# The low half of the split weights: a negated copy on ScalarE and an accumulating DMA in place of VectorE's subtraction

## The chip, the core and the metric

The kernel runs on one core of one Trainium2 chip. The metric is the time of one execution on the device, in microseconds (us); lower is better. One execution was recorded by the hardware profiler, and its times of single instructions are used here. Instruction times, windows and starts are counted from the first instruction of that execution.

The engines go by the names of the profile: PE is TensorE (PEld its weight loads), DVE is VectorE, ACT is ScalarE, POOL is GpSimd, SP is SyncE, which here only issues DMAs.

## The reference

A linear recurrence over 768 steps of time for 4 batches and 8 heads of 48 channels, and a dense layer with GELU behind it:

```python
for t in range(S):
    kt, vt, rt = (k[:, :, t], v[:, :, t], r[:, :, t])
    cur = np.einsum('bhd,bhe->bhde', u[None] * kt, vt)
    y[:, :, t] = np.einsum('bhd,bhde->bhe', rt, state + cur)
    state = w[None, :, :, None] * state + np.einsum('bhd,bhe->bhde', kt, vt)
x = y.transpose(0, 2, 1, 3).reshape(B * S, H * D)      # 3072 x 384
h = x @ w_in                                           # 384 x 2048, float64
g = 0.5 * h * (1.0 + erf(h * inv_sqrt2))
out = (g @ w_out).astype(np.float32)                   # 2048 x 384, float64
```

The two weight matrices come as 64-bit floats. The kernel turns them into 32-bit floats on the chip, and splits each into a high half that TensorE's fp32r format holds and a low half that is the rest.

## The kernel before

**Tiling.** Time is cut into 6 tiles of 128 steps; a tile holds 4 batches x 128 steps = 512 tokens (`TOK`). The hidden dimension of the dense layer is cut into 16 blocks of 128 (`NJ`). So the dense layer has 6 x 16 = 96 steps `m`, of which the first 16 (tile 0) run while the weights are still being prepared. The recurrence is done in 24 groups, 6 tiles x 4 pairs of heads; groups 0 to 3 come first, the others are spread over the steps, one group to four steps.

**One step of the dense layer** (`moe1` and `moe2`, the matmuls in lines 602 and 642). `product1` makes `Hp` = w_in block times x in nine matmuls of 128 x 512: three with the high weights `wh` and the high half of x, three with the low weights `wl`, three with `wh` and the low half of x. ScalarE reads `Hp` twice, L630 writes `gh` (GELU, rounded to fp32r) and L631 writes `gf` (GELU in 32 bits); VectorE makes `gl = gf - gh` in L632. `product2` adds nine more matmuls into the banks `O0` to `O2`: `wh` with `gh`, `wl` with `gh`, `wh` with `gl`.

**The weights** (`w_load` and `w_split`), once for each of the 16 blocks, in tile 0 alone; the results stay in SBUF for all tiles. SP loads block `j` into `raw` (three buffers, 128 x 768 values of 64 bits, L317). ScalarE makes the magnitude from the high word (L330, into `wa`, three buffers) and converts the low word (L332, into `wb`, two buffers). VectorE shifts (L334), sets the sign (L336) and adds the low bits (L338); then `wa` holds the 32-bit weights. ScalarE copies them into `wh` (L340, the write rounds to fp32r), and VectorE subtracts: `wl = wa - wh` (L342). The next user of the same `wa` buffer is L330 of block `j + 3`.

**A group of the recurrence** (`prepare`, `products`, `state`, `past_scores`, `finish`): SP loads `Tb` (L208) and `Nb` (L212); VectorE scales `Tb` (L479) and sums (L491); POOL multiplies `Nb` three times (L482, L485, L488); TensorE runs L519, L527, L536 and L546; ScalarE writes `Am` in eight pieces of 128 x 64 (L351) and the high half of x (L367); VectorE updates the states (L569), selects (L576) and writes the low half of x (L368). `Nb` has two buffers; the load of one waits for the matmuls of L546 of the group that used it, two groups before.

**What sets the order.** The class `Plan` takes every operation with an engine, a cost in nanoseconds and a due time, plays them through once at build time, and writes each engine's queue in the order in which its model starts them: the ready operation that is due first. Each queue then runs in that fixed order on the chip; an instruction whose input is late holds up all that stand behind it on its engine. An operation whose due time is `LATER` inherits it from those that need it. So a change of one operation's engine or cost reorders the queues of all engines.

Of the kernel before, what the change touches and what calls it, by code (L numbers as in the profile page):

```python
# [9 lines left out]
F32 = mybir.dt.float32  # L10
# [3 lines left out]
AF = mybir.ActivationFunctionType  # L14
ALU = mybir.AluOpType
# [20 lines left out]
LATER = 10 ** 7  # L36
# [10 lines left out]
class Plan:  # L47
# [9 lines left out]
    def add(self, eng, ns, at, fn, r=(), w=()):  # L57
        n = len(self.ops)
        deps = set()
        for x in r:  # L60
            deps.add(self.writer.get(x))
            self.readers.setdefault(x, []).append(n)
        for x in w:
            deps.add(self.writer.get(x))
            deps.update(self.readers.pop(x, ()))
            self.writer[x] = n
        deps -= {None, n}
        self.ops.append((eng, ns, at, fn, deps))
        self.reads.append(set(r))
# [65 lines left out]
def rwkv_gelu_mlp(tc, rkT, rkv, wuT, uN, wmlp, r, k, vT, w, u, out):  # L135
    nc = tc.nc
    with ExitStack() as ctx:
# [7 lines left out]
        def sb(shape, dt, name, pool=None):  # L145
            return (pool or wk).tile(shape, dt, name=name)
# [11 lines left out]
        wh = [sb([128, 2, DM], F32R, f"wh{j}", cst) for j in range(NEAR)]  # L158
        wl = [sb([128, 2, DM], F32R, f"wl{j}", cst) for j in range(NEAR)]
# [33 lines left out]
        add, dma = plan.add, plan.dma  # L193
        dve = lambda n: 65 + n / 0.96
        dve2 = lambda n: 65 + n / 1.92
        act = lambda n: 95 + n / 1.2
        sdve = lambda n: 145 + n / 0.96
        sdve2 = lambda n: 145 + n / 1.92
        sact = lambda n: 225 + n / 1.2
        pool = lambda n: 110 + n * 2.15  # L200
# [28 lines left out]
        for dst, src, x in ((diag2, diag, "diag"), (past2, past, "past")):  # L229
            for h in range(2):  # L230
                add("act", 280, LATER, lambda dst=dst, src=src, h=h: nc.scalar.copy(
                    out=dst[64 * h:64 * h + 64], in_=src[64 * h:64 * h + 64, 64 - 64 * h:128 - 64 * h]),
                    r=[x], w=[f"{x}2{h}"])
# [86 lines left out]
        def w_split(j):  # L320

            a, b = wa[j % 3], wb[j % 2]
            A_, B_, R_ = f"wa{j % 3}", f"wb{j % 2}", f"raw{j % 3}"
            bits = raw[j % 3].rearrange("p h n t -> p (h n) t")
            lo, hi = bits[:, :, 0], bits[:, :, 1]
            af = a.bitcast(F32)
            gate = ["late"] if j >= NEAR else []
            n = 2 * DM
            both = lambda w: w[j].rearrange("p h n -> p (h n)")
            add("act", sact(n), LATER, lambda: nc.scalar.activation(out=af, in_=hi.bitcast(F32), func=AF.Abs,  # L330
                                                                scale=2.0 ** -112), r=[R_], w=[A_])
            add("act", sact(n), LATER, lambda: nc.scalar.activation(out=b, in_=lo.bitcast(U32), func=AF.Copy,  # L332
                                                                scale=2.0 ** -29), r=[R_], w=[B_])
            add("dve", sdve2(n), LATER, lambda: nc.vector.tensor_scalar(  # L334
                out=a, in0=a, scalar1=3, scalar2=None, op0=ALU.logical_shift_left), w=[A_])
            add("dve", sdve(n), LATER, lambda: nc.vector.scalar_tensor_tensor(  # L336
                out=a, in0=hi, scalar=-2 ** 31, in1=a, op0=ALU.bitwise_and, op1=ALU.bitwise_or), r=[R_], w=[A_])
            add("dve", sdve(n), LATER, lambda: nc.vector.tensor_tensor(out=a, in0=a, in1=b, op=ALU.add),  # L338
                r=[B_], w=[A_])
            add("act", sact(n), LATER, lambda: nc.scalar.copy(out=both(wh), in_=af), r=[A_] + gate,  # L340
                w=[f"wh{2 * j}", f"wh{2 * j + 1}"])
            add("dve", sdve(n), LATER, lambda: nc.vector.tensor_tensor(  # L342
                out=both(wl), in0=af, in1=both(wh).bitcast(F32), op=ALU.subtract),
                r=[A_, f"wh{2 * j}", f"wh{2 * j + 1}"] + gate, w=[f"wl{2 * j}", f"wl{2 * j + 1}"])


        def bonus(am, AM, diag, DIAG, n, sums, CS, j, e):
# [432 lines left out]
        for G in range(NSTEP + 1):  # L780
            if 0 <= G < NJ:
                if G >= 3:
                    w_load(G, step_at(G) - WEIGHT_AHEAD)
                w_split(G)
            if G < NSTEP:
                moe1(G, step_at(G))
            if G == 0:
                group(NP, LATER)
            if G % 4 == 0 and G // 4 + NP < NG:
                gi = G // 4 + NP + 1  # L790
                at = step_at(4 * (gi - 1 - NP)) + GROUP_DUE
                if 5 < gi < NG:
                    load_group(gi, at - GROUP_AHEAD)
                group(gi, at)
            if G >= 1:
                moe2(G - 1, step_at(G) + 2000, out[(G - 1) // NJ])
            if G == 2 * NJ:
                count_plain(step_at(G))
# [96 lines left out]
```

## Time and profile before

| | |
|---|---|
| median of 3 runs | 512.32 us (511.55 to 515.15) |
| the profiled execution | 512.43 us, of which 510.7 us is the span from the first to the last instruction |
| PE busy | 488.2 us, 96% of the span |
| PEld busy | 387.8 us, 76% |
| DVE busy | 248.8 us, 49% |
| ACT busy | 213.6 us, 42% |
| POOL busy | 88.6 us, 17% |
| mean granted TensorE clock | 0.973 |

The shares are means over stages that differ. Up to about 34 us the first four groups and the first weights are prepared; from there to about 127 us the 16 steps of tile 0 run beside the preparation of the weights; after that TensorE runs steps from weights that are all in SBUF. In a row of a group of instructions stand line, engine, operation, output and inputs with their shapes, the count, then the total busy time, the mean of one in ns, and the idle time of the engine before them with what ended it. In a row of a window stand its bounds, its length and the busy time of PE, PEld, DVE, ACT and POOL (with the number of instructions), the granted clock, the share of the DMA engines and GB/s. In a row of the timeline stand start, duration, engine, line and operation.

### The profile page before, as it was taken

How to read it: one execution, taken by the hardware profiler on the slowest of the kernel's cores; microseconds unless marked ns; L12 is line 12 of the kernel's file. 1: busy time of each engine (PE TensorE's matmuls, PEld its weight loads, DVE VectorE, ACT ScalarE, POOL GpSimd, SP SyncE). 2: the span in 40 equal slices, each digit the busy share in tenths (PEclk: the TensorE clock that was granted, in tenths of full speed). 3: DMA queues.
4: the chain of work that ended last, by engine and by line, in shares of the span. 5: the costliest groups of instructions: out<-in, count | busy, mean ns of one | idle time of the engine just before them, and what ended most of it. 6: DMA issues, size and time to landing. Idle time of an engine off the chain costs nothing.

```text
span 510.7 us, 10489 instructions
## 1 busy us (share of the span) xinstructions
PE 488.2 (96%) x4524; PEld 387.8 (76%) x4524; DVE 248.8 (49%) x363; ACT 213.6 (42%) x472; POOL 88.6 (17%) x80
## 2 busy tenths in 40 slices
PE   5998898999999999999999999999999999999995
PEld 4876676766778778787777778778778787888884
DVE  8959999998536424614425435424424311211111
ACT  2458758774444243333343443343442322322221
POOL 5850311213022022202022022022022000000000
PEclk8659999999999999999999999999999999999998
DMA  8864574822402303403302403303403000100001
GB/s 226 254 251 145 189 231 149 252 83 63 145 7 89 94 4 92 145 1 94 95 1 94 142 5 94 94 1 94 134 13 94 13 0 12 62 1 0 1 0 67
DMA packets 15107, 45.04 MB, mean 88 GB/s; under 512 B 3728, under 2 KB 4112, under 8 KB 15056
## 3 DMA queue, kind: packets, MB, share of 16 engines
q1 hardware_dynamic: 15056, 44.32, 27.8%
q8 instruction: 37, 0.61, 0.5%
q14 instruction: 14, 0.11, 0.1%
HBM read 37.16 MB, written 4.72 MB: 82 GB/s over the span
## 4 chain that ended last, share of the span: by engine, by line
PE 84%; DVE 11%; issue 2%; ACT 1%; DMA 1%; SPq 0%; DVEq 0%
PE Hp L602 37%; PE O L642 35%; PE Y L546 2%; PE Y L519 2%; PE A L527 2%; DVE wa L338 1%; DVE wl L342 1%; DVE Ts L393 1%; PE A L536 1%; PE Y L642 1%; DVE gl L632 1%; DVE wa L336 1%; DMA T<-in_rkT_dram 1%; DVE wa L334 1%; ACT wh L340 1%
## 5 line engine op out<-in xcount | busy, mean ns | idle before, releaser
L602 PE MATMUL Hp<-xx,wh 128*128 128x512 f32 x576 | 168.8, 400 | 0.8 <-ACT gf L631 0.5
L632 DVE TENSOR_TENSOR gl<-gf,gh 128x512 fp32r<-128x512 f32 x95 | 73.2, 770 | 193.9 <-ACT gf L631 193.8
L630 ACT ACTIVATE gh<-Hp 128x512 fp32r<-128x512 f32 x95 | 56.7, 597 | 183.6 <-PE Hp L602 183.5
L602 PEld LDWEIGHTS Hp<-xx,wh 128*128 128x128 f32 x576 | 105.8, 188 | 26.6 <-ACT gf L631 1.5
L642 PE MATMUL O<-gh,wh 128*128 128x512 f32 (+1 forms) x285 | 82.0, 395 | 6.2 <-ACT gh L630 6.2
L602 PE MATMUL Hp<-xx,wl 128*128 128x512 f32 x288 | 84.1, 399 | 0.7 <-DVE wl L342 0.3
L642 PE MATMUL O<-gh,wl 128*128 128x512 f32 (+1 forms) x285 | 80.8, 391 | 0.0
L642 PE MATMUL O<-gl,wh 128*128 128x512 f32 (+1 forms) x285 | 80.6, 390 | 0.0
L482 POOL TENSOR_TENSOR Nb<-Nb 128x384 f32<-128x384 f32 x20 | 22.6, 1131 | 294.9 <-DMA Nb<-in_rkv_dram 257.5
L642 PEld LDWEIGHTS O<-gh,wh 128*128 128x128 f32 x285 | 52.6, 188 | 23.4 <-ACT gh L630 11.9
L602 PEld LDWEIGHTS Hp<-xx,wl 128*128 128x128 f32 x288 | 53.5, 188 | 15.6 <-DVE wl L342 3.3
L642 PEld LDWEIGHTS O<-gl,wh 128*128 128x128 f32 x285 | 52.6, 188 | 11.9 <-DVE gl L632 0.2
L642 PEld LDWEIGHTS O<-gh,wl 128*128 128x128 f32 x285 | 52.6, 188 | 11.7
L351 ACT ACTIVATE Am<-diag,cs 128x64 f32<-128x64 f32 (+1 forms) x176 | 47.4, 345 | 22.8 <-DVE cs L491 22.7
L631 ACT ACTIVATE gf<-Hp 128x512 f32<-128x512 f32 x96 | 56.9, 593 | 0.0
L367 ACT CAST xx<-Y 112x512 fp32r<-112x512 f32 (+1 forms) x16 | 9.4, 587 | 41.7 <-PE Y L546 41.0
L479 DVE TENSOR_TENSOR Tb<-Tb,E 112x1024 f32<-112x1024 f32 x20 | 24.4, 1220 | 2.9 <-DMA Tb<-in_rkT_dram 2.9
L488 POOL TENSOR_TENSOR Nb<-Nb,u_sb 128x384 f32<-128x384 f32 x20 | 25.6, 1282 | 0.2
L569 DVE SCALAR_TENSOR_TENSOR Sb<-Sa,E,A 48x192 f32<-48x192 f32 x40 | 16.5, 413 | 16.0 <-PE A L536 15.4
L485 POOL TENSOR_TENSOR Nb<-Nb,WN 128x384 f32<-128x384 f32 x20 | 22.7, 1135 | 2.7 <-ACT WN L293 1.3
L576 DVE COPY_PREDICATED Am<-past,A 128x512 f32<-128x512 uint32 x20 | 14.8, 738 | 7.0 <-PE A L536 6.8
L342 DVE TENSOR_TENSOR wl<-wa,wh 128x768 fp32r<-128x768 f32 x16 | 16.7, 1042 | 1.9 <-ACT wh L340 1.7
(114 smaller groups left out, 396.1 us busy)
## 6 DMA issues: line engine op xcount, KB each, us to landing
raw<-in_wmlp_dram SPq DMA_DIRECT2D x16, 768.0 KB, 6.9
Nb<-in_rkv_dram SPq DMA_DIRECT2D x20, 576.0 KB, 5.4
Tb<-in_rkT_dram SPq DMA_DIRECT2D x20, 448.0 KB, 3.9
out_dram<-raw SPq DMA_DIRECT2D x5, 768.0 KB, 4.6
xx<-x SPq DMA_DIRECT2D x30, 64.0 KB, 3.9
T<-in_rkT_dram SPq DMA_DIRECT2D x4, 448.0 KB, 6.9
N<-in_rkv_dram SPq DMA_DIRECT2D x4, 384.0 KB, 9.5
out_dram<-raw SPq DMA_DIRECT2D x2, 256.0 KB, 2.8
```

The source lines that it names most:

```text
L342: add("dve", sdve(n), LATER, lambda: nc.vector.tensor_tensor(out=both(wl), in0=af, in1=both(wh).bitcast(F32), op=ALU.subtract), r=[A_, f"w ...
L351: add("act", sact(n) + 90, LATER, lambda b=b: nc.scalar.activation(out=am[:, j, b, :], in_=diag, func=AF.Copy, scale=sums[:, 2 * b + j:2 * ...
L479: add("dve", sdve(1024), LATER, lambda: nc.vector.tensor_tensor(out=flat, in0=flat, in1=E[:, 0, p].rearrange("l h i -> l (h i)").unsqueeze ...
L482: add("pool", pool(DM), LATER, lambda: nc.gpsimd.tensor_tensor(out=n[:, 0], in0=n[:, 0], in1=n[:, 1], op=ALU.mult), r=[NK], w=[NR])
L485: add("pool", pool(DM), LATER, lambda: nc.gpsimd.tensor_tensor(out=kn, in0=kn, in1=WN2[:, p].rearrange("s j d -> s (j d)").unsqueeze(1).to ...
L488: add("pool", pool(DM), LATER, lambda: nc.gpsimd.tensor_tensor(out=n[:, 0], in0=n[:, 0], in1=u_sb[:, p, :].unsqueeze(1).to_broadcast([C, N ...
L569: add("dve", 420, at, lambda l=l, x=x: nc.vector.scalar_tensor_tensor(out=out[quarter(1 - x)], in0=src[l], scalar=E[l, 1, p, h, 32:33], in ...
L602: nc.tensor.matmul(Hp, lhsT=wt[j][:, 0, k_ * 128:(k_ + 1) * 128], rhs=x[:, a, k_, :], start=start and k_ == ks[0], stop=stop and k_ == ks[-1])
L630: add("act", 480, LATER, lambda: nc.scalar.activation(out=high, in_=Hp, func=AF.Gelu), r=["H"], w=[GH])
L631: add("act", 480, LATER, lambda: nc.scalar.activation(out=gf, in_=Hp, func=AF.Gelu), r=["H"], w=["gf"])
L632: add("dve", dve(512), LATER, lambda: nc.vector.tensor_tensor(out=low, in0=gf, in1=high.bitcast(F32), op=ALU.subtract), r=["gf", GH], w=[GL])
L642: nc.tensor.matmul(dst[:, a:b], lhsT=wt[j][:, 1, d * 128:(d + 1) * 128], rhs=gt[:, a:b], start=(j == 0 and n == 0), stop=(j == NJ - 1 and ...
```

## The change

In `w_split` the subtraction on VectorE (L342) is taken out. Two operations take its place: ScalarE writes the negative of `wa` into `wl` (the write rounds to fp32r, so that it is exactly `-wh`), and POOL issues a DMA from `wa` to `wl` that adds to what stands there (384 KB; source and destination both in SBUF). `wl` is then `wa - wh` as before. The negated copy needs `wa` alone and no longer `wh`. The DMA is entered in the plan as 3500 ns of POOL.

```diff
             add("act", sact(n), LATER, lambda: nc.scalar.copy(out=both(wh), in_=af), r=[A_] + gate,
                 w=[f"wh{2 * j}", f"wh{2 * j + 1}"])
-            add("dve", sdve(n), LATER, lambda: nc.vector.tensor_tensor(
-                out=both(wl), in0=af, in1=both(wh).bitcast(F32), op=ALU.subtract),
-                r=[A_, f"wh{2 * j}", f"wh{2 * j + 1}"] + gate, w=[f"wl{2 * j}", f"wl{2 * j + 1}"])
+
+            add("act", sact(n), LATER, lambda: nc.scalar.activation(out=both(wl), in_=af, func=AF.Copy, scale=-1.0),
+                r=[A_] + gate, w=[f"wl{2 * j}", f"wl{2 * j + 1}"])
+            add("pool", 3500, LATER, lambda: nc.gpsimd.dma_start(out=both(wl).bitcast(F32), in_=af, accum_op=ALU.add),
+                r=[A_], w=[f"wl{2 * j}", f"wl{2 * j + 1}"])
```

Lines below the edit move down by two, so L482 is L484 in the changed kernel, L602 is L604, L630 is L632. The negated copy is L343, the DMA L345.

The queues are reordered by it. On ScalarE, around the steps 2 and 3 of tile 0 (`wh2` and `wh3` are the high weights of blocks 2 and 3, `gh1_126` and `gh0_125` the GELUs of steps 1 and 2), the queue before reads:

```order
L330 ACTIVATE wa1_134<-raw1_131 128x768
L630 ACTIVATE gh1_126<-Hp_69 128x512
L631 ACTIVATE gf_129<-Hp_69 128x512
L351 ACTIVATE Am1_115<-diag2_85,cs1_119 128x64
L340 CAST wh2_76<-wa2_135 128x768
L332 ACTIVATE wb0_136<-raw1_131 128x768
L351 ACTIVATE Am1_115<-diag2_85,cs1_119 128x64 x5
L340 CAST wh3_77<-wa0_133 128x768
L630 ACTIVATE gh0_125<-Hp_69 128x512
```

and that of the change, in the same place (`wl2` and `wl3` are the negated copies):

```order
L343 ACTIVATE wl2_80<-wa2_135 128x768
L340 CAST wh2_76<-wa2_135 128x768
L632 ACTIVATE gh1_126<-Hp_69 128x512
L633 ACTIVATE gf_129<-Hp_69 128x512
L330 ACTIVATE wa1_134<-raw1_131 128x768
L343 ACTIVATE wl3_81<-wa0_133 128x768
L340 CAST wh3_77<-wa0_133 128x768
L332 ACTIVATE wb0_136<-raw1_131 128x768
L330 ACTIVATE wa2_135<-raw2_132 128x768
L632 ACTIVATE gh0_125<-Hp_69 128x512
```

The preparation of a block stands one place more ahead of the GELUs than before: between the negated copy of block 2 and the GELU of step 2 (the last row) stand eight instructions. Further down, at step 6, the queue of the change has:

```order
L343 ACTIVATE wl6_434<-wa0_133 128x768
L340 CAST wh6_433<-wa0_133 128x768
L332 ACTIVATE wb0_136<-raw2_132 128x768
L353 ACTIVATE Am0_114<-diag2_85,cs0_118 128x64
L343 ACTIVATE wl7_436<-wa1_134 128x768
L340 CAST wh7_435<-wa1_134 128x768
L332 ACTIVATE wb1_137<-raw0_130 128x768
L343 ACTIVATE wl8_438<-wa2_135 128x768
L632 ACTIVATE gh0_125<-Hp_69 128x512
```

Here three negated copies stand ahead of the GELU of step 6 (last row). On POOL, which before had only the multiplications of the groups here, the 16 DMAs now stand among them; around blocks 3 to 8 its queue reads (`Nb0` and `Nb1` are the two buffers of the groups):

```order
L345 DMA wl3_81<-wa0_133 128x768
L484 TENSOR_TENSOR Nb0_112<-Nb0_112 128x384
L487 TENSOR_TENSOR Nb0_112<-Nb0_112,WN2_93 128x384
L345 DMA wl4_430<-wa1_134 128x768
L345 DMA wl5_432<-wa2_135 128x768
L490 TENSOR_TENSOR Nb0_112<-Nb0_112,u_sb_82 128x384
L484 TENSOR_TENSOR Nb1_113<-Nb1_113 128x384
L345 DMA wl6_434<-wa0_133 128x768
L345 DMA wl7_436<-wa1_134 128x768
L345 DMA wl8_438<-wa2_135 128x768
L487 TENSOR_TENSOR Nb1_113<-Nb1_113,WN2_93 128x384
```

The DMAs of blocks 4 and 6 stand right behind the first multiplications of a group, which wait for that group's load of `Nb`. On SP one weight load changes places with the two loads of a group; else the loads of tile 0 keep their order. On PE the first product of tile 0 stands behind three more of the idle matmuls of line 249.

## The prediction

> **What bounds the kernel now.** I read first the windows: the stage in which the weights are prepared (34 to 127 us), and what follows.
>
> ```profile
> core 0: us, PE busy (x) PEld busy (x) DVE busy (x) ACT busy (x) POOL busy (x), PEclk, DMA share, GB/s
> 34.00:127.00 93.00, 84.85 (x920) 61.64 (x920) 87.76 (x118) 67.16 (x127) 20.32 (x14) 0.99 0.47 153
> 130.00:500.00 370.00, 367.96 (x3383) 297.29 (x3382) 131.33 (x201) 128.48 (x299) 45.83 (x42) 1.00 0.18 56
> ```
>
> From 130 us on TensorE is busy 368.0 of 370 us; nothing that the change touches runs there. In the stage VectorE is busy 87.8 of 93 us (94%) and ScalarE 67.2 (72%), and TensorE has holes. The chain of work that ended last shows who sets the end of the stage:
>
> ```profile
> 120.81 1.70 DVE wa L338
> ...
> 124.23 0.96 DVE wl L342
> 125.23 1.67 PE Hp L602 x6
> ...
> 153.50 2.30 PE Hp L602 x9
> ...
> 172.78 2.31 PE Hp L602 x9
> ```
>
> The last subtraction (L342) ends at 125.2 us, and the product of step 15 starts with it. The last two rows are one place in the queue four steps and one group apart: 19.28 us, or 4.82 us a step, is TensorE's own pace. Sixteen steps at it would be 77 us, 75 up to the GELU of step 15, and they took about 90. So this stage has some 13 us to give, and no other has any.
>
> **What goes.** VectorE loses sixteen subtractions:
>
> ```profile
> L342 DVE TENSOR_TENSOR wl<-wa,wh 128x768 fp32r<-128x768 f32 x16 | 16.7, 1042 | 1.9 <-ACT wh L340 1.7
> ```
>
> That leaves 87.8 - 16.7 = 71.1 us for VectorE, below TensorE's 75: VectorE bounds no longer. What is gained depends on what ends last instead.
>
> **ScalarE's own work.** It gets sixteen copies. Its pace I take from starts that follow each other without a wait, not from durations, which overlap:
>
> ```profile
> 32.89 0.58 ACT L367 CAST xx<-Y 128x512 fp32r<-128x512 f32 x1 [0.68 <-PE Y L445]
> 33.37 0.64 ACT L450 COPY Sa<-Y 48x192 f32<-48x192 f32 x2
> 34.03 0.83 ACT L340 CAST wh<-wa 128x768 fp32r<-128x768 f32 x1
> 34.77 0.91 ACT L332 ACTIVATE wb<-raw 128x768 int32<-128x768 uint32 x1
> ...
> 40.01 2.02 ACT L351 ACTIVATE Am<-diag,cs 128x64 f32<-128x64 f32 x8
> ...
> 43.34 0.60 ACT L630 ACTIVATE gh<-Hp 128x512 fp32r<-128x512 f32 x1
> 43.83 0.59 ACT L631 ACTIVATE gf<-Hp 128x512 f32<-128x512 f32 x1
> 44.30 0.89 ACT L330 ACTIVATE wa<-raw 128x768 f32<-128x768 f32 x1
> 45.10 0.91 ACT L332 ACTIVATE wb<-raw 128x768 int32<-128x768 uint32 x1
> ...
> 126.94 0.60 ACT L630 ACTIVATE gh<-Hp 128x512 fp32r<-128x512 f32 x1 [0.81 <-PE Hp L602]
> ```
>
> A cast to `wh` takes 0.73 us to the next start, L330 and L332 0.80, a GELU 0.49 and 0.48, a piece of `Am` 0.24, L367 0.50, L450 0.33. The new copy is an activation with a scale over 128x768 like L330: 0.80 (0.73 if it goes like the cast, 1.1 us less in all). From the first cast at 34.03 to the GELU of step 15 at 126.94 are 92.9 us; by these figures ScalarE works 63.3 of them. In the changed order there stand, from the first negated copy to that GELU, 16 copies, 16 casts, 15 L332, 14 L330, 15 pairs of GELUs, 40 pieces, 5 L367 and 6 L450: 12.8 + 11.7 + 12.0 + 11.2 + 14.6 + 9.6 + 2.5 + 2.0 = 76.3 us. That is below 92.9, and about as long as TensorE's own 75. With no waits at all the stage would be some 16 us shorter.
>
> **The wait that the change adds.** The low weights now come by DMA: negated copy, POOL, transfer, then TensorE. The GELU of step j cannot start before that and the six matmuls behind it, and ScalarE's queue stands still behind that GELU. TensorE's part, from the last `wl` arriving to the GELU:
>
> ```profile
> 125.23 0.97 PE L602 MATMUL Hp<-xx,wl 128*128 128x512 f32 x3 [0.35 <-DVE wl L342]
> 126.04 0.86 PE L602 MATMUL Hp<-xx,wh 128*128 128x512 f32 x3
> ```
>
> 125.23 to 126.94: 1.7 us. The latency of the DMA is not in this trace, which has no DMA from POOL and none that adds. The nearest rows, first over the whole span, the large outputs among them with the DMA engines nearly idle, then for 34 to 126 us:
>
> ```profile
> out_dram<-raw SPq DMA_DIRECT2D x5, 768.0 KB, 4.6
> ...
> out_dram<-raw SPq DMA_DIRECT2D x2, 256.0 KB, 2.8
> ```
>
> ```profile
> raw<-in_wmlp_dram SPq DMA_DIRECT2D x12, 768.0 KB, 5.9
> Nb<-in_rkv_dram SPq DMA_DIRECT2D x4, 576.0 KB, 5.2
> ...
> xx<-x SPq DMA_DIRECT2D x6, 64.0 KB, 6.8
> ```
>
> The issue on POOL costs at least what SP's does and at most what POOL's multiplications take here:
>
> ```profile
> 46.30 0.33 SPq L208 DMA_DIRECT2D Tb<-in_rkT_dram  x1
> 47.96 0.33 SPq L212 DMA_DIRECT2D Nb<-in_rkv_dram  x1
> ```
>
> ```profile
> 35.01 1.00 POOL L488 TENSOR_TENSOR Nb<-Nb,u_sb 128x384 f32<-128x384 f32 x1
> 53.56 1.43 POOL L482 TENSOR_TENSOR Nb<-Nb 128x384 f32<-128x384 f32 x1 [17.55 <-DMA Nb<-in_rkv_dram]
> 55.07 1.62 POOL L485 TENSOR_TENSOR Nb<-Nb,WN 128x384 f32<-128x384 f32 x1
> ```
>
> Lower bound: 384 KB as a plain transfer on idle engines, between 2.8 and 4.6, so 3.25 us, plus 0.33 and 0.1 for a semaphore: 3.7 us. Upper bound: the transfer reads the destination too, so it counts as 768 KB, and runs beside the weight loads: 6.8 (the slowest row of the stage, a copy within SBUF), plus 1.6 and 0.2: 8.6 us. I take the 576 KB row of the stage, 5.2, which lies between plain and twice read, plus 0.7 for the issue and 0.1: **6.0 us**. With TensorE's 1.7 that is 7.7 us from the end of a negated copy to the GELU of its step.
>
> The Trainium skill, "DMA: Bandwidth & Descriptors", section "Anatomy of one DMA — SWDGE (gpsimd) path", fits 2.0 us plus bytes over 436 GB/s to a DMA from GpSimd: 2.9 us for these 393,216 bytes, 3.8 with the second read counted. Its 3.8 for 768 KB stands against 4.6 in the row of the quiet outputs. By it the latency would be near my lower bound, which is the first rival below.
>
> Now I walk down ScalarE's changed queue with those paces. Between the end of the negated copy of step j and its GELU stand, in us of work: step 2 5.6, step 4 5.2, step 6 4.9, step 10 5.1, step 13 6.1, step 14 4.4, step 15 2.7; the others are covered, having 5.5 to 8.7, or a stall inside their window makes them so. Each short window stalls by the rest of 7.7: 2.1 + 2.6 + 2.8 + 2.6 + 1.6 + 3.3, and 1.8 for step 15 (the stall of step 14 lies in its window): 16.8 us. 76.3 + 16.8 = 93.1 us, against 92.9 before: **+0.2**. The gain on VectorE is paid back to the DMA's latency. At the start the first product waits for the DMA (34.8 + 6.0 = 40.8 us; it began at 37.6), but the first GELU is due on ScalarE at 43.1 anyway: no cost.
>
> **POOL's queue.** DMAs that stand behind a group's multiplications wait for that group's `Nb`. In the rows above SP issued the load at 47.96 and POOL began at 53.56: 5.6 us, then 1.4 to 1.6 for each multiplication. In the walk the copy of block 4 ends at 58.0 and its two multiplications at 56.7 by the trace of before, in time or up to 0.8 late. For block 6 the copy ends at 72.9; its `Nb1` is free after the products behind the GELU of step 4 (65.7 in the walk, so about 67.5), and 5.6 + 1.6 later it is 74.7: 1.8 late, in a short window. Block 11 is late in the same way by about 0.7. Together **+3.3**.
>
> **What costs nothing.** The weight loads: three `raw` buffers, each held for a landing of 5.9 us and some 5 us of L330 to L336, feed a block every 3.6 us where 5.8 are used; a landing could double before it shows. The weight load that passes two group loads on SP, for the same reason. The next L330 into a `wa` buffer waits for the DMA to have read it, but stands 5 us or more behind, beside the same stalls. Behind 127 us nothing changes.
>
> The sum: 512.43 (the profiled execution, 0.1 above the median of the runs) + 0.2 + 3.3 = **515.9 us**. A measurement can tell about 1% (5.1 us) from no change.
>
> **The rivals.** *The DMA is quick* (3.7 us, so 5.4 in all): the walk gives 80.1 us, 12.8 less; two queues that are each some 76 us long won't both run without holes (VectorE, with 87.8 us of work, took 93), so 5 come back: 504.5. For it speak the quiet outputs; against it the slower rows of the stage. *The DMA is slow*: the walk costs some 7 us for each us of latency, since five or six windows are short. It goes past +1% at about 6.3 us; at 7.6 us (raw's 5.9 for twice 384 KB plus the longest issue) the walk gives 104.2, +11.3, with POOL's +3.3 some 527; at the upper bound, 8.6, 112 and 535. For it speaks the copy within SBUF, 64 KB in 6.8 us. *The transfers collide*: the added reads delay the weight loads until they bind; at twice 5.9 us the stage gets some 6 us longer, 519. Against it, the slack of a landing above. That the change does not do what it says, a stage that stays as it is because TensorE holds it, gives 512.4 and lies inside my own case.
>
> **How the numbers follow.** Forecast, latency 5.4 to 6.6 us: 0.40, own range 509 to 521. Quick 0.22, slow 0.30, colliding 0.08. Faster by over 1%: 0.19 of the quick case, 0.02 of my own: 0.21. Slower by over 1%: 0.29 of the slow, 0.05 of the colliding, 0.10 of my own: 0.44. Within 1%: 0.35. The range reaches from the quick case to beyond the middle of the slow one: 504 to 531.
>
> **What would show it.** Right: VectorE's busy time falls by some 17 us and it waits in the stage; ScalarE works about 13 us more; the waits name ScalarE's GELU behind L602, and TensorE's L602 behind the DMA into `wl`, most at steps 2, 4, 6, 10 and 14; the landing stands near 5.3 us. From the end of the stage the two traces run alike, shifted by the difference. Wrong: landings under 4 us, with ScalarE or TensorE busy through the stage and an end 8 us earlier; landings of 7 or more; or POOL long busy with each issue, so that the DMAs queue on POOL itself.

## The result, and the profile after

The changed kernel takes 539.62 us (median of four runs, 535.4 to 542.06) against 513.74 us for the kernel before beside it: ratio 1.050, 95% interval 1.0453 to 1.0547. It is slower by 5%, and above the range of the prediction, which ended at 531. The profiled execution took 535.4 us, the fastest of the four, of which 533.6 us are the span, 22.9 us more than before. The numbers below are from it.

The page of the changed kernel first: busy times, the matmuls with the low weights with what ended the idle time before them, and the landing of the added DMA.

```profile
PE 492.9 (92%) x4527; PEld 392.9 (74%) x4527; DVE 237.0 (44%) x347; ACT 224.0 (42%) x488; POOL 100.6 (19%) x96
...
L604 PE MATMUL Hp<-xx,wl 128*128 128x512 f32 x288 | 87.6, 412 | 21.4 <-DMA wl<-wa 21.4
...
wl<-wa POOLq DMA_DIRECT2D x16, 384.0 KB, 6.9
```

VectorE does 11.8 us less in all (237.0 for 248.8) and ScalarE 10.4 more (224.0 for 213.6). TensorE now waits 21.4 us for the added DMA. The window of the stage in the same kernel, in the form of those of before:

```profile
34.00:150.00 116.00, 89.81 (x862) 67.09 (x866) 75.25 (x100) 72.39 (x134) 30.02 (x29) 0.85 0.67 175
```

The GELU of step 15 stood at 126.94 us and stands at 149.99 us, 23.05 us later, which is the whole difference of the spans. So 34 to 127 us before compares with 34 to 150 us after. (The steps of this execution also begin earlier: the GELU of step 0 stands at 40.33 us, before at 43.34. From there to the GELU of step 15 are 83.6 us before and 109.7 us after, 26.1 more, as much as lies between the two medians, 25.9.) In it TensorE is idle for 26.2 us where it was 8.2 (18.0 more), and busy for 89.8 where it was 84.9 (5.0 more) at a granted clock of 0.85 for 0.99. 18.0 + 5.0 = 23.0: more waiting, and slower matmuls. VectorE is no bound any more (75.3 of 116), and neither is ScalarE (72.4).

From step 1 on, the chain of waits of the changed kernel goes through the DMA at four steps (start, us, what):

```profile
46.48 0.75 ACT wl L343
47.23 0.29 issue
47.52 9.59 DMA wl<-wa
...
57.16 2.94 PE Hp L604 x6
...
73.74 5.10 DMA Nb<-in_rkv_dram
...
78.90 3.13 POOL Nb L484
82.03 7.23 DMA wl<-wa
...
89.31 2.94 PE Hp L604 x6
...
107.81 9.25 DMA wl<-wa
...
117.11 2.94 PE Hp L604 x6
...
139.16 3.92 DMA wl<-wa
```

These are steps 2, 6, 10 and 14. In the first three the DMA lands 7.2 to 9.6 us after its issue, and the six matmuls behind it take 2.94 us, where they took 1.67 before. (Ahead of them the chain also holds the DMA of block 0, which lands at 36.0 us; the GELU of step 0 comes 3.0 us earlier than before all the same.) At step 14, when the weight loads are over, it lands after 3.9. The timeline of ScalarE shows what stands still behind the three long ones (start, duration, line; the wait in brackets):

```profile
57.19 0.90 ACT L330 ACTIVATE wa<-raw 128x768 f32<-128x768 f32 x1 [4.90 <-issue]
60.12 0.60 ACT L632 ACTIVATE gh<-Hp 128x512 fp32r<-128x512 f32 x1 [2.04 <-PE Hp L604]
...
78.56 0.85 ACT L343 ACTIVATE wl<-wa 128x768 fp32r<-128x768 f32 x1
81.06 0.85 ACT L343 ACTIVATE wl<-wa 128x768 fp32r<-128x768 f32 x1
83.30 0.85 ACT L343 ACTIVATE wl<-wa 128x768 fp32r<-128x768 f32 x1
92.27 0.60 ACT L632 ACTIVATE gh<-Hp 128x512 fp32r<-128x512 f32 x1 [8.12 <-PE Hp L604]
...
106.67 0.84 ACT L343 ACTIVATE wl<-wa 128x768 fp32r<-128x768 f32 x1
...
120.08 0.60 ACT L632 ACTIVATE gh<-Hp 128x512 fp32r<-128x512 f32 x1 [7.62 <-PE Hp L604]
```

From the end of the negated copy to the GELU of its own step are 12.9 us at steps 2 (47.23 to 60.12) and 6 (79.41 to 92.27) and 12.6 at step 10 (107.51 to 120.08). Step 6 shows the order at work: the copies of blocks 6, 7 and 8 all stand ahead of that GELU, three DMAs go out within 3 us, and the one that is waited for is among them.

### The profile page after: what moved, and what is told of

The parts are those of the page before. It is cut to its first block, busy times and chain, and to the rows that moved or that the text cites. A ratio compares the mean times of both kernels' runs of the same rounds, so it can differ in the third digit from the quotient of the medians.

```text
span 533.6 us, 10534 instructions
## 1 busy us (share of the span) xinstructions
PE 492.9 (92%) x4527; PEld 392.9 (74%) x4527; DVE 237.0 (44%) x347; ACT 224.0 (42%) x488; POOL 100.6 (19%) x96
## 4 chain that ended last, share of the span: by engine, by line
PE 82%; DMA 9%; POOL 3%; issue 2%; ACT 2%; DVE 0%; SPq 0%; POOLq 0%
PE Hp L604 38%; PE O L644 35%; DMA wl<-wa 7%; PE Y L548 3%; PE Y L521 2%; PE A L529 2%; PE A L538 1%; PE Y L644 1%; DMA Nb<-in_rkv_dram 1%; POOL N L413 1%; DMA T<-in_rkT_dram 1%; POOL Nb L484 1%; POOL RK L401 1%; ACT gh L632 1%; POOL Ts L395 1%
## 5 line engine op out<-in xcount | busy, mean ns | idle before, releaser
L604 PE MATMUL Hp<-xx,wh 128*128 128x512 f32 x576 | 172.7, 408 | 0.0
L634 DVE TENSOR_TENSOR gl<-gf,gh 128x512 fp32r<-128x512 f32 x95 | 70.7, 744 | 228.8 <-ACT gf L633 228.7
L632 ACT ACTIVATE gh<-Hp 128x512 fp32r<-128x512 f32 x95 | 56.8, 598 | 199.6 <-PE Hp L604 199.3
L604 PEld LDWEIGHTS Hp<-xx,wh 128*128 128x128 f32 x576 | 108.9, 194 | 26.2 <-ACT wh L340 0.5
L604 PE MATMUL Hp<-xx,wl 128*128 128x512 f32 x288 | 87.6, 412 | 21.4 <-DMA wl<-wa 21.4
L604 PEld LDWEIGHTS Hp<-xx,wl 128*128 128x128 f32 x288 | 55.9, 196 | 36.8 <-DMA wl<-wa 23.7
L484 POOL TENSOR_TENSOR Nb<-Nb 128x384 f32<-128x384 f32 x20 | 23.9, 1196 | 239.3 <-DMA Nb<-in_rkv_dram 162.2
L644 PEld LDWEIGHTS O<-gh,wh 128*128 128x128 f32 x285 | 53.8, 191 | 19.9 <-ACT gh L632 7.4
L644 PEld LDWEIGHTS O<-gh,wl 128*128 128x128 f32 x285 | 53.0, 190 | 11.8
L481 DVE TENSOR_TENSOR Tb<-Tb,E 112x1024 f32<-112x1024 f32 x20 | 30.2, 1512 | 1.1 <-DMA Tb<-in_rkT_dram 1.0
L345 POOL DMA_DIRECT2D wl<-wa x16 | 14.2, 925 | 69.6 <-ACT wl L343 40.6
```

What stands on the lines that cost most here:

```text
L481: add("dve", sdve(1024), LATER, lambda: nc.vector.tensor_tensor(out=flat, in0=flat, in1=E[:, 0, p].rearrange("l h i -> l (h i)").unsqueeze ...
L484: add("pool", pool(DM), LATER, lambda: nc.gpsimd.tensor_tensor(out=n[:, 0], in0=n[:, 0], in1=n[:, 1], op=ALU.mult), r=[NK], w=[NR])
L604: nc.tensor.matmul(Hp, lhsT=wt[j][:, 0, k_ * 128:(k_ + 1) * 128], rhs=x[:, a, k_, :], start=start and k_ == ks[0], stop=stop and k_ == ks[-1])
L632: add("act", 480, LATER, lambda: nc.scalar.activation(out=high, in_=Hp, func=AF.Gelu), r=["H"], w=[GH])
L634: add("dve", dve(512), LATER, lambda: nc.vector.tensor_tensor(out=low, in0=gf, in1=high.bitcast(F32), op=ALU.subtract), r=["gf", GH], w=[GL])
L644: nc.tensor.matmul(dst[:, a:b], lhsT=wt[j][:, 1, d * 128:(d + 1) * 128], rhs=gt[:, a:b], start=(j == 0 and n == 0), stop=(j == NJ - 1 and ...
```

## The experiments

All ratios are against the kernel before, run on the same chip in the same rounds.

### ScalarE's copies without the DMA

```diff
-            add("pool", 3500, LATER, lambda: nc.gpsimd.dma_start(out=both(wl).bitcast(F32), in_=af, accum_op=ALU.add),
+            add("dve", sdve(n), LATER, lambda: nc.vector.tensor_tensor(
+                out=both(wl), in0=af, in1=both(wl).bitcast(F32), op=ALU.add),
```

> ScalarE's part alone: it still writes the negated copy, but VectorE adds the weights on top (one 128x768 operation per block, as in the kernel before), and there is no DMA from POOL. Theory (the DMA's latency in ScalarE's and TensorE's queues costs the time): near the kernel before, 510 to 520 us, TensorE waits for no DMA in the stage. Rival (ScalarE's sixteen extra copies cost it): 528 us or more with ScalarE busy over 85% of the stage.

Measured: 514.95 us, ratio 1.0027 (0.9991 to 1.0063). This is the theory's range. The sixteen copies on ScalarE cost nothing that can be told; the loss comes with the DMA, by its wait or by the order that is made around it.

### The DMA without the adding

```diff
-            add("pool", 3500, LATER, lambda: nc.gpsimd.dma_start(out=both(wl).bitcast(F32), in_=af, accum_op=ALU.add),
+            add("pool", 3500, LATER, lambda: nc.gpsimd.dma_start(out=both(wl).bitcast(F32), in_=af),
```

> The DMA from POOL copies and does not add, so that the low weights are the whole ones; all else as in the change, the order too. Theory (the transfer shares the 16 DMA engines with the weight loads and is slow while one runs): it moves only a third less, the landings beside a weight load stay above 6 us, and the time is 530 to 540 us. Rival (adding to the destination is what makes it slow): all landings under 5 us, the time 525 us or less.

Measured: 527.87 us, ratio 1.0272 (1.0197 to 1.0347). Two views of the tile `wl` in this kernel, the issue on POOL (ns, least, median, most) and the landing:

```profile
L345 POOL DMA_DIRECT2D wl<-wa x16: 538/579/708, 30.5 to 133.9; - x16
...
DMA to landing us min/median/max: 2.6/5.7/7.9
```

and the same in the changed kernel:

```profile
L345 POOL DMA_DIRECT2D wl<-wa x16: 850/870/1178, 29.7 to 142.1; - x16
...
DMA to landing us min/median/max: 3.9/6.9/10.7
```

The time lies between the two expectations. By the medians of the sixteen the adding makes each DMA 1.2 us slower, a quarter of that on POOL; from 34 to 127 us, where the weights are loaded, it is 2.5 us (8.5 for 6.0). By the medians of the times the adding is 12 of the 26 us. The rest is there with a plain copy too.

### The order made with the real latency

```diff
-            add("pool", 3500, LATER, lambda: nc.gpsimd.dma_start(out=both(wl).bitcast(F32), in_=af, accum_op=ALU.add),
+            add("pool", 900, LATER, lambda: nc.gpsimd.dma_start(out=both(wl).bitcast(F32), in_=af, accum_op=ALU.add),
                 r=[A_], w=[f"wl{2 * j}", f"wl{2 * j + 1}"])
+            plan.late[len(plan.ops) - 1] = 7000
```

`plan.late` is a table of the latencies, in ns, that the plan adds between an operation and those that read its result.

> The planner is told what the trace of the change shows: POOL is busy 900 ns with an issue, and the low weights are there 7000 ns later; nothing else is changed, so the order of the queues differs. Theory that only the planner's 3500 ns made the wait: back to 508 to 520 us. Rival (the wait itself stays, since ScalarE's and TensorE's queues have too little other work while the transfer and the weight loads share the DMA engines): 525 us or more, TensorE still waiting over 10 us for these DMAs.

Measured: 522.81 us, ratio 1.0195 (1.0129 to 1.0261). The waits of TensorE's weight loads for the DMA from 34 to 165 us (total, times, longest), in the changed kernel and in this one:

```profile
PEld Hp L604 <- DMA wl<-wa: 23.7, 6, 8.6
...
PEld Hp L608 <- DMA wl<-wa: 3.6, 3, 2.9
```

Nearly all of TensorE's wait for the DMA is gone (3.6 us for 23.7), and the landings from 34 to 127 us have a median of 4.8 us where the change has 8.5. The order is worth some 16 of 26 us; the plan was told a shorter time on POOL and a longer latency at once, and the two were not tried apart. The time lies between the two expectations: about 2% stays. The chain of this kernel still holds one long landing, 9.4 us at step 2.

### Weight loads with a quarter of the bytes

```diff
-            dma(128 * 6144, at, lambda: nc.sync.dma_start(raw[j % 3].rearrange("p h n t -> p (h n t)"), wbits[:, j]),
-                w=[f"raw{j % 3}"])
+            q = 4 * DM if j < 3 else DM
+            dma(128 * 6144, at, lambda: nc.sync.dma_start(
+                raw[j % 3].rearrange("p h n t -> p (h n t)")[:, 0:q], wbits[:, j, 0:q]), w=[f"raw{j % 3}"])
```

> From block 3 on, each weight load brings a quarter of its bytes (the rest of the buffer keeps the words of an earlier block); the order and all else as in the change. Theory of the shared DMA engines: median landing of the adding DMA near 4 us instead of 6.9, no landing above 6 after the first, the time 510 to 522 us. Rival (the adding DMA is slow by itself, or POOL is): landings stay at 6 or more, the time 530 us or more.

Measured: 525.15 us, ratio 1.0219 (1.0147 to 1.0291). The DMA issues of this kernel from 34 to 127 us and, behind them, its chain of waits at step 6:

```profile
wl<-wa POOLq DMA_DIRECT2D x13, 384.0 KB, 4.3
raw<-in_wmlp_dram SPq DMA_DIRECT2D x12, 192.0 KB, 3.3
```

```profile
71.12 5.41 DMA Nb<-in_rkv_dram
...
76.60 2.81 POOL Nb L485
79.41 3.94 DMA wl<-wa
...
83.39 2.94 PE Hp L605 x6
```

The landings fall from 8.5 to 4.3 us, while VectorE and POOL have the work of the changed kernel (75.7 and 31.6 us from 34 to 140 us, 75.3 and 30.0 there from 34 to 150): what makes them long is the weight loads beside them. That is worth some 14 us. But the forecast for this run missed: with a quick landing the kernel is still 2.2% slower than before. In the chain the DMA of block 6 still goes out behind the multiplication that waits for `Nb`, and TensorE still drops to 2.94 us behind the wait.

### TensorE kept busy while it waits

At steps 2, 6 and 10 the first three matmuls (with `wh`) are repeated 6, 10 and 6 times.

```diff
-                    add("pe", 3 * 216, at + n, lambda n=n: product1(x, j, n, start=n == 0, stop=n == 2),
+                    add("pe", 3 * 216, at + n, lambda n=n: [
+                        product1(x, j, 0, start=True, stop=True) for _ in range({2: 6, 6: 10, 10: 6}.get(m, 0) * (n == 0))]
+                        + [product1(x, j, n, start=n == 0, stop=n == 2)],
```

> The change, with TensorE kept at work in its three long waits: the three matmuls of the high weights at steps 2, 6 and 10 are done 6, 10 and 6 times more, each starting the sum afresh, so the result and the order stay. Theory (a part of the loss is that TensorE's granted clock falls while it waits, and the matmuls behind the wait run slowly): the nine to fifteen matmuls behind these waits take 0.23 us each instead of up to 0.43, the clock stays at 0.95 or more, and the time falls by 4 to 9 us, to about 531 to 535. Rival (the slow matmuls do not count, the waits alone do): 537 to 543 us.

Measured: 534.63 us, ratio 1.0373 (1.0286 to 1.0459). The timeline of TensorE at the low weights of steps 2, 6 and 10 in this kernel:

```profile
63.98 0.86 PE L604 MATMUL Hp<-xx,wl 128*128 128x512 f32 x3
...
95.41 0.96 PE L604 MATMUL Hp<-xx,wl 128*128 128x512 f32 x3 [1.86 <-DMA wl<-wa]
...
121.41 0.97 PE L604 MATMUL Hp<-xx,wl 128*128 128x512 f32 x3 [0.50 <-DMA wl<-wa]
```

and in the changed kernel:

```profile
57.16 1.65 PE L604 MATMUL Hp<-xx,wl 128*128 128x512 f32 x3 [4.83 <-DMA wl<-wa]
...
89.31 1.65 PE L604 MATMUL Hp<-xx,wl 128*128 128x512 f32 x3 [8.16 <-DMA wl<-wa]
...
117.11 1.65 PE L604 MATMUL Hp<-xx,wl 128*128 128x512 f32 x3 [5.25 <-DMA wl<-wa]
```

Three matmuls take 0.86 to 0.97 us when TensorE had work, and 1.65 after it stood for 5 to 8 us. The granted clock shows the same. In the changed kernel it is 0.50 while the six matmuls of step 6 run:

```profile
89.31:92.25 2.94, 2.92 (x6) 1.81 (x6) 0.00 (x0) 0.00 (x0) 0.00 (x0) 0.50 0.91 175
```

Here it is 1.00 over those of the same step (95.41 to 97.09 us). By the medians the kernel gains 5 us, as much as TensorE's busy time grew (5.0), and lands in the theory's range; the two intervals touch. The two profiled spans are alike (533.9 and 533.6), because the steps begin later in this one: the GELU of step 0 stands at 46.62 us and that of step 15 at 150.43. From the one to the other are 103.8 us here and 109.7 in the changed kernel, so the stage is 5.9 us shorter.

### VectorE relieved without a DMA

```diff
-            add("dve", sdve(n), LATER, lambda: nc.vector.tensor_tensor(
+            add("pool", 2400, LATER, lambda: nc.gpsimd.tensor_tensor(
                 out=both(wl), in0=af, in1=both(wh).bitcast(F32), op=ALU.subtract),
```

> The kernel before, with the subtraction of the low weights moved from VectorE to POOL (one operation of 128x768, told to the planner as 2400 ns) and no DMA. Theory (taking the work from VectorE is right, and only the way by DMA is too long): at 2.0 to 3.3 us an operation the low weights come earlier than by DMA, 500 to 512 us. Rival (POOL and VectorE hold each other up, as the longer durations of both in the stage show): VectorE's operations get longer, no gain or a loss, 514 to 525 us.

Measured: 516.85 us, ratio 1.0033 (0.9986 to 1.0079). The kernel before with the subtraction on POOL, one window of the stage:

```profile
60.00:80.00 20.00, 17.64 (x194) 13.87 (x194) 19.62 (x23) 14.00 (x26) 11.32 (x7) 1.00 0.56 176
```

The rival's range holds. VectorE is rid of 1.04 us a block and is busy 98% of these 20 us all the same (94% of them before, with POOL busy 4.53 us): its setting of the sign (L336) takes 1354 ns here and 985 before, the shift 841 for 603, while POOL has more work beside it. So VectorE is not relieved in this way.

### The DMAs alone, with nobody waiting for them

```diff
+            add("pool", 900, LATER, lambda: nc.gpsimd.dma_start(
+                out=spare, in_=af[:, 0:640], **(dict(accum_op=ALU.add) if j else {})), r=[A_], w=["spare"])
```

> The kernel before, with VectorE's subtraction, and 16 adding DMAs from POOL of 128x640 into a spare tile that nobody reads, one per block. Theory (the latency in the chain of the low weights is what costs): the DMAs' traffic and POOL's issues alone cost little, 513 to 519 us, though landings are 4 to 9 us and the next block in the same buffer waits for them now and then. Rival (the added traffic delays the weight loads, or POOL's issues delay the groups): 525 us or more.

Measured: 530.97 us, ratio 1.032 (1.0229 to 1.041): the theory's range fell and the rival's holds; which cause it has, the time alone does not show. The waits of this kernel name the buffer:

```profile
POOL spare L347 <- DMA spare<-wa: 14.8, 5, 3.7
ACT wa L332 <- DMA spare<-wa: 10.7, 4, 3.4
```

L332 here is the magnitude (L330 of before). It waits for its `wa` buffer until the DMA has read it, and the GELUs stand behind it in ScalarE's queue. One spare tile also makes each adding DMA wait for the one before. So this run pointed to the held buffer, as in the 4.90 us of L330 above. The next two runs put that to the test.

```diff
-                out=spare, in_=af[:, 0:640], **(dict(accum_op=ALU.add) if j else {})),
-                r=[A_], w=["spare"])
+                out=spare, in_=both(wh).bitcast(F32)[:, 0:640], **(dict(accum_op=ALU.add) if j else {})),
+                r=[A_, f"wh{2 * j}", f"wh{2 * j + 1}"], w=["spare"])
```

> The kernel before with the sixteen adding DMAs into a spare tile of the run in which they cost 18 us without a reader (531 us), but each now reads the high half of its own block, which is never written again, and not wa: the same bytes and the same line of one DMA behind another on the spare tile, and no buffer held. Theory (what cost 18 us was the hold of wa): 513 to 518 us, and L332 waits for no DMA. Rival (the traffic and the POOL queue cost it, through later weight loads and later multiplications on POOL): 524 to 531 us.

Measured: 516.76 us, ratio 1.0053 (1.0013 to 1.0093). The same DMAs that hold no buffer cost half a per cent. L332 waits for none of them. In that pair the hold was 14 of the 18 us (each DMA also waits for the copy into `wh` here); the traffic and POOL's queue were the small rest.

### The change with nothing held

```diff
-            add("pool", 3500, LATER, lambda: nc.gpsimd.dma_start(out=both(wl).bitcast(F32), in_=af, accum_op=ALU.add),
+            add("pool", 3500, LATER, lambda: nc.gpsimd.dma_start(out=both(wl).bitcast(F32),
+                in_=wh[j - 1].rearrange("p h n -> p (h n)").bitcast(F32) if j else af, accum_op=ALU.add),
```

> The changed kernel, in which the adding DMA of every block but the first reads the high half of the block before (a tile that is never written again) and not wa, so the buffer wa comes free with the third VectorE operation and the two copies and is no longer held for 4 to 10 us. Bytes, queue, issue, order and the wait of the low weights are the same. The low weights become wrong numbers, so only the time counts. Theory (the held buffer is a second path of the loss, beside the wait for the low weights: line L330 waited 4.9 us for a buffer at 57.2 us, with the GELUs behind it in ScalarE's queue): it ends 5 to 10 us below the changed kernel, 529 to 535 us. Rival (only the wait of TensorE for the low weights counts, the held buffer stands beside the same stalls): 536 to 541 us, the three long waits of TensorE at the low weights unchanged.

Measured: 540.61 us, ratio 1.0486 (1.0422 to 1.0549): the rival's range held. The timeline of TensorE at steps 2, 6 and 10 in this kernel:

```profile
63.22 0.97 PE L604 MATMUL Hp<-xx,wl 128*128 128x512 f32 x3 [3.05 <-DMA wl<-wh]
...
95.51 1.65 PE L604 MATMUL Hp<-xx,wl 128*128 128x512 f32 x3 [8.84 <-DMA wl<-wh]
...
123.49 1.65 PE L604 MATMUL Hp<-xx,wl 128*128 128x512 f32 x3 [5.41 <-DMA wl<-wh]
```

L330 no longer waits. Two of the three long waits of TensorE are as in the changed kernel (8.16 and 5.25 there), the first is shorter (4.83 there), and ScalarE stands 4.24 us at the GELU of step 2, where it stood 4.90 at L330 and 2.04 at the GELU. The time is the same, and so is the way from the GELU of step 0 to that of step 15 (109.5 us for 109.7): in the change the held buffer stands beside the wait for the low weights, which takes its place. What the idle DMAs cost was a cost of that experiment and not a second part of the loss.

### POOL's queue emptied

The three multiplications of `Nb` go to VectorE, once with the change's order and once with the known latency.

```diff
-            add("pool", pool(DM), LATER, lambda: nc.gpsimd.tensor_tensor(
+            add("dve", sdve(DM), LATER, lambda: nc.vector.tensor_tensor(
                 out=n[:, 0], in0=n[:, 0], in1=n[:, 1], op=ALU.mult), r=[NK], w=[NR])
...
```

> The changed kernel with the three multiplications of each later group on Nb (lines L484, L487, L490; about 1.0 to 1.3 us each on POOL) on VectorE, so POOL's queue holds nothing but the adding DMAs and none is issued behind a multiplication that waits for its load. VectorE has 41 of 116 us idle from 34 to 150 us in the changed kernel and takes about 0.55 us for each. Theory (the DMAs of blocks 6 and 11 left 2.6 and about 1 us late behind L484 and its load): 3 to 5 us below the changed kernel, 534.5 to 537 us. Rival (the landing beside weight loads decides, the issue does not; or VectorE now waits for the same loads with the weights' steps behind it): 538 to 543 us.

> The kernel whose order is made with a latency of 7 us for the adding DMA (522.8 us), with the multiplications on Nb on VectorE as in the run beside it. Theory (what is left of the loss there comes from DMAs and multiplications that hold each other up in POOL's queue, such as the 8.6 us wait of L488 ahead of the DMA at 104.1 us): 515 to 519 us. Rival (what is left is the traffic beside the loads, 5.7 to 9.4 us to land): 521 to 526 us; above that if VectorE, which has 32 of 116 us idle there, becomes the bound.

Measured: 537.01 us, ratio 1.047 (1.0416 to 1.0523), and 518.87 us, ratio 1.0129 (1.008 to 1.0178). The first lies between the two expectations, 3 us under the change and inside its interval; TensorE's weight loads wait as long for the DMA as in the change (23.7 us):

```profile
PEld Hp L604 <- DMA wl<-wa: 24.7, 6, 7.3
```

At step 6, where the DMA had stood behind L484, TensorE's matmuls now wait 2.7 us instead of 8.2; but at steps 2 and 10 they wait 6.3 and 6.9 instead of 4.8 and 5.2, and step 8 is new with 1.9.

The second is 4 us under the run with the known latency (522.81), as the theory had it, though the intervals overlap. By the medians POOL's queue is worth some 3 to 4 us, which neither pair shows beyond its intervals.

### The DMA for a part of the blocks

In the first run the odd blocks, in the second the blocks 2, 5, 8, 11 and 14 (`j % 3 == 2`) go by negated copy and adding DMA with the known latency; the others go by VectorE as before.

```diff
+            if j % 2:
+                add("act", sact(n), LATER, lambda: nc.scalar.activation(out=both(wl), in_=af, func=AF.Copy, scale=-1.0),
+                    r=[A_] + gate, w=[f"wl{2 * j}", f"wl{2 * j + 1}"])
+                add("pool", 900, LATER, lambda: nc.gpsimd.dma_start(out=both(wl).bitcast(F32), in_=af, accum_op=ALU.add),
+                    r=[A_], w=[f"wl{2 * j}", f"wl{2 * j + 1}"])
+                plan.late[len(plan.ops) - 1] = 7000
+            else:
...
```

> The odd blocks get their low weights by negated copy and DMA, with the planner told 900 ns of POOL and 7000 ns of latency, the even blocks by VectorE's subtraction. Theory (half of VectorE's relief is worth half the gain, and the latency can be hidden for half of the blocks): 506 to 514 us. Rival (each DMA beside a weight load stops ScalarE's queue once, whatever the planner knows): 515 to 520 us.

> The kernel of which every second block went by negated copy and adding DMA with the known latency (512.15 us, 0.996 of the kernel before), now with five of sixteen blocks (2, 5, 8, 11, 14) by DMA and eleven by VectorE. If what an added DMA costs by its hold and its traffic outweighs the 1.05 us of VectorE that it saves, fewer DMAs are better: 510 to 512 us. If VectorE's work is what the saving comes from and the hold is covered at every second block, fewer DMAs give less: 512.5 to 514 us, level with before.

Measured: 512.15 us, ratio 0.996 (0.9923 to 0.9997), and 520.5 us, ratio 1.0118 (1.0076 to 1.0159). With every second block by DMA the kernel is level with before, or faster by a few tenths of a per cent; it is the best that was found, inside the theory's range. With five blocks both expectations missed. The chain of that kernel shows one place:

```profile
103.31 4.23 POOL Nb L498
107.54 5.51 DMA wl<-wa
...
113.10 2.94 PE Hp L612 x6
```

The DMA of block 11 stands behind a multiplication of `Nb`, and the matmuls behind it take 2.94 us again, at a granted clock of 0.50. Why this order loses 8 us more than that with eight DMAs was not tried further and stays open.

## Why the prediction was wrong

**What bounds the kernel: right.** Nothing but the stage of the weights changed; from the GELU of step 15 on the traces run alike, shifted by 23.05 us (the steps began 3.0 us earlier, and took 26.1 longer). **ScalarE is no bound: right**, it works 72.4 of 116 us, and its copies cost nothing (514.95).

**The latency of 6.0 us: the first of two steps that failed.** It was taken from the 576 KB row of the stage, between a plain copy and one read twice. The issues of the changed kernel from 34 to 127 us:

```profile
raw<-in_wmlp_dram SPq DMA_DIRECT2D x12, 768.0 KB, 6.6
wl<-wa POOLq DMA_DIRECT2D x12, 384.0 KB, 8.5
```

8.5 us, with 0.3 ahead of the issue 8.8, just above the upper bound of 8.6, for which the prediction had 535 us; the profiled execution took 535.4. From the end of a negated copy to the GELU of its step are 12.6 to 12.9 us at steps 2, 6 and 10, where the prediction had 7.7. The mistake was to price the DMA as a load of its size in the average of the stage. It goes out beside the next weight loads, and together with the DMAs of its neighbours. SP's weight loads wait for L336, VectorE's last reading of a `raw` buffer, and behind L336 of a block only L338 and the negated copy follow before its DMA goes out: SP issued weight loads at 47.94, 81.29 and 108.83 us, POOL the DMAs of steps 2, 6 and 10 at 47.52, 82.03 and 107.81. The windows of the changed kernel over the transfers of steps 2, 6, 10 and 14 (the last three columns are the granted clock, the share of the DMA engines and GB/s):

```profile
47.50:57.10 9.60, 4.83 (x21) 3.57 (x19) 8.89 (x11) 4.57 (x7) 4.36 (x4) 0.88 0.97 248
82.00:89.30 7.30, 0.00 (x0) 0.00 (x0) 2.95 (x4) 2.15 (x3) 4.60 (x6) 0.74 1.02 265
107.80:117.00 9.20, 3.52 (x14) 2.19 (x13) 6.17 (x9) 4.66 (x8) 5.51 (x6) 0.96 1.02 304
139.10:143.10 4.00, 3.58 (x15) 2.25 (x13) 3.90 (x5) 4.00 (x11) 3.04 (x4) 1.00 0.65 119
```

The DMA engines are full in the three long ones, and not in the short one. The run with quarter loads confirms it: 4.3 us. The order counts too: in the one made for the real latency the same DMAs landed after 4.8 us beside full loads.

**TensorE's 1.7 us: too small.** Behind a wait of 5 to 8 us the six matmuls take 2.94 us, 1.27 more, three times 3.8 of the 5.0 us by which TensorE's busy time grew. No term of the sum held this, since the trace of before has no such wait there.

**The walk down ScalarE's queue: the second step that failed; its places half right, its base too low.** It named steps 2, 4, 6, 10, 13, 14 and 15, with stalls of 1.6 to 3.3 us. Three of them, 2, 6 and 10, carry the loss: 2.0 (and 4.9 at L330 ahead of it), 8.1 and 7.6 us. Steps 4, 13 and 14 stall 1.2, 0.9 and 1.6, and 3, 11 and 15, not named or named with less, 2.4, 3.4 and 3.8. "Five or six short windows, 7 us for each us" was too steep too: from 4.3 to 8.5 us of landing the time moves by 14.5 us (525.15 to 539.62), some 3.4 us for each. And with 4.3 us, 4.6 with the way to the issue, the walk would have given about 511 with POOL's part (between the 504.5 at 3.7 and the 512.6 at 6.0, plus 3.3), while the run shows 525. So the walk was low by 14 us where the DMA is quick, and its agreement at 8.6 us is in part two errors that cancel. By these figures, an estimate, of the 23.7 us between the forecast and the median (515.9 and 539.62) some 10 go to the latency and some 14 to the walk.

The term that the walk put at nothing is ScalarE's other waiting. It adds 16.8 us of stalls for the DMA to 76.3 us of work, and so lets ScalarE wait for nothing else, without a reason (only the quick rival got 5 us back for holes); but by the same paces ScalarE had worked only 63.3 of its 92.9 us before. The waits at the GELUs (total, times, longest), before from 34 to 127 us and in the changed kernel from 34 to 150:

```profile
ACT gh L630 <- PE Hp L602: 14.5, 13, 2.6
...
ACT gh L632 <- PE Hp L604: 33.5, 14, 8.1
```

The 14.5 us of before stand there without any DMA, and with quarter loads it is still 22.7. To them come the low clock behind waits (some 5 us) and 3.1 us in which L343 waits for VectorE. No run takes these waits away, so how they share the 14 us is not shown. The quick rival, 504.5, would not have come true even with the quick landing.

**POOL's +3.3: right in kind.** The DMA of block 6 went out 2.6 us behind its copy (predicted 1.8), since L484 waited for `Nb` and took 3.1 us; moving these multiplications away cut TensorE's wait at step 6 from 8.2 to 2.7 us and the whole by 2.6 us in the change and 4 with the known latency, neither beyond the intervals.

**"What costs nothing": right.** The held `wa` buffer shows as a wait of 4.9 us and yet costs nothing in the change (540.61 with it free). **VectorE's -16.7 us** came out as 11.8 in all, since some other lines grew (the scaling of `Tb` from 1220 to 1512 ns, L336 from 985 to 1136); it decided nothing.

**The slow rival** is what happened: landings of 7 us or more, waits named at steps 2, 6 and 10. It had 0.30, and the range stopped short of its end.

**The planner's 3500 ns** is the condition under all of it. The order was made for a result 3.5 us after the start on POOL, and the negated copies were set close to the GELUs that need them. Told 7 us, the same operations lose 2% and not 5.

Open stays what the last 1.3 to 2% of the kernel with the known latency is, beside POOL's queue and the one long landing, and why five DMAs lose more than eight.

## What to carry to other kernels

Price a new transfer by the windows in which it will be issued, not by the mean of its stage: look at the DMA share at the moment when its input is ready, because the step that makes it ready may have freed a load buffer just before, as here. Whoever walks down a queue should count the waits that the trace of before already has in it. When an order is planned from costs, a wrong latency there can cost more than the operation itself; correct it before judging the change. A wait that the profile names is not yet a cost: take it away and see whether another wait steps into its place, as with the held buffer here.

## What the runs showed of the hardware

- An adding DMA of 384 KB within SBUF, issued by POOL, landed after 3.9 us once the weight loads were over, after 8.5 us (median from 34 to 127 us) beside them, 10.7 at most; in the order made for the real latency the median beside them was 4.8. As a plain copy it took 2.6 us at best and 6.0 in the median from 34 to 127 us. POOL was held 0.87 us by each issue, 0.58 for the plain one. The Trainium skill, "DMA: Bandwidth & Descriptors", section "Anatomy of one DMA — SWDGE (gpsimd) path", by its fit gives an estimate of 2.9 us, 3.8 with the second read counted; the quietest landings here, 2.6 of the plain copy and 3.9 of the adding one, lie near them, and the 8.5 beside the loads does not.
- TensorE after a wait of 5 to 8 us ran three matmuls of 512 columns in 1.65 us; after a wait of under 2 us, 0.95 to 0.97 us. After waits of about 3 us both were seen: 0.97 us behind 3.05 (the change with nothing held, step 2), 1.65 behind 2.71 (POOL's queue emptied, step 6). The granted clock was 0.50 behind the long waits and 1.00 behind the waits that repeated matmuls had filled.
- More work on POOL made VectorE's instructions longer: with POOL busy 11.3 of 20 us, L336 took 1354 ns for 985 and the shift 841 for 603. In the change L336 took 1136 ns and the scaling of `Tb` 1512; with POOL's multiplications moved to VectorE, 987 and 1221.
